# A recurrent attention and SoLU feed-forward kernel gets a new written-out order of work: u spread by a bf16 product, no dummy products, more loads issued by GpSimd, more transposes by DMA

## The chip, the cores and the metric

The kernel runs on one core of a Trainium2 chip. The metric is the device time of one execution in microseconds (us); the time of a kernel is the median of its runs. A core has five engines that run beside one another, each through its own list of instructions in order: PE (TensorE, products), DVE (VectorE), ACT (ScalarE), POOL (GpSimd) and SP (SyncE, which here only issues transfers). PEld in the profile is PE's loading of weights. Transfers (DMA) are issued from SP, ACT or POOL. PSUM is the memory that PE writes to, in eight banks; POOL does not read it here.

## The reference, cut to what matters

```
B, H, S, D = 4, 8, 768, 48                       # batch, heads, sequence, head width
for t in range(S):                               # recurrence, for each b, h
    cur = (u * k[t]) outer v[t]
    y[t] = r[t] @ (state + cur)
    state = w[t][:, None] * state + k[t] outer v[t]
x = y as rows of 384 (8 heads x 48), 3072 of them
h = x @ w_in                                     # 384 -> 1024
solu = h * softmax(h)                            # along 1024
ln = (solu - mean) / sqrt(var + 1e-6) * g_ln     # along 1024
out = ln @ w_out                                 # 1024 -> 384, float32
```

## The kernel before, in words

The sequence is cut into 6 chunks of 128 steps; a chunk of one batch entry is a unit, so there are 24 units, numbered chunk by chunk (units 0 to 3 are the first chunk of the four batch entries). All eight heads of a unit are handled together; rows are the 128 steps.

A unit goes through these stages, each a small function with a two- or three-letter word (line numbers of the kernel before in brackets):

- Loads of w, k, r, v, 192 KB each: `LW`, `LK`, `LR`, `LV` (264 to 275), into rings of seven buffers (`NIO`).
- `lw` takes the logarithm of w on ACT (338); `cum` sums it along the steps by two products on PE (341); `ex` is the exponential on ACT, in place in PSUM (347); `kp` scales k and r by it on DVE (351).
- `krk` and `krr` turn k and r by eight transposes on PE (380), and `kr` copies them from PSUM on ACT or DVE (395). `kt` does all of this by one DMA transpose issued from SP (399).
- `M` forms the scores by eight products (408), `m` copies them and cuts them to the lower triangle on DVE, or copies them on ACT and leaves the triangle to POOL's `sel` (416, 425).
- The u term: `p` = k times r and `q` = p times u on POOL (355, 359), `dg` sums q over a head on DVE (372), `dv` = v times dg on POOL (376). `vb` is v in bf16, by ACT or POOL (368).
- `Y` is the attention output: products with the state of the chunk before and with v (430). With `.i` an identity product on PE adds dv and `y` is a copy on ACT; with `.n` the addition is part of `y` on DVE (452).
- `S` forms the state's increment (458), `et` its decay on ACT, `st` the new state on DVE (482). With `S.n` an identity product that adds the old state is left out and `st` is two DVE instructions, a sum and a product.
- `X` and `xT` turn y by three transposes and a copy (491, 496); `xt` does it by a DMA transpose from SP (402).
- `H` is the hidden product (503), `e` its exponential on ACT, `he` the product of both on DVE, `hq` its square, mostly on ACT. Units named by an `ht` word have the hidden product by rows, and a DMA turns their result (405).
- `Oa`, `Ob` are the output product (584): for each of eight blocks one product of 386 columns with the prepared w_out, one of two columns with e and one of one column with hq. `ea` and `qa` (529, 550) let POOL add the two halves of e or of hq first, so that four small products do for eight.
- `qm`, `lv`, `rs` form the scale of a row, `o` applies it on ACT or DVE, `out` stores 192 KB from SP (630 to 665). Unit 23's hidden stage is split in halves (`HA`, `HB` and so on, 554).

Once, at the start, come: `us`, `uc`, u as a row spread over 128 partitions by an fp32 product and copied (290, 294); `gs`, `gc`, the gain turned (297); `wi`, w_in in bf16 (304); `gw`, `mn`, `mc`, `ce`, w_out times the gain, its column mean, and the mean taken off (308 to 328); `ih`, `ik`, constants made by POOL (243, 255); and `hot`, dummy products of 512 columns that nobody reads (330).

The order of the work is written out in one string, `ORDER` (line 21), of some 880 words: stage, number, and after a dot how it is done. For loads this is the queue (none: SP, `a`: ACT, `g`: POOL), for computing stages the engine (`a`, `d`, `p`) or the PSUM bank. The words are run one after another (line 680), and each engine's instructions stand in the order in which the words name them, loads included:

```
queue = {"": sp, "a": act, "g": pool}
...
for word in ORDER.split():
    word, _, how = word.partition(".")
    name = word.rstrip("0123456789")
    stages[name](int(word[len(name):]), how)
```

Every instruction is recorded through one helper, so nearly all have line 86 in the profile; they are told apart by tiles: `kp`, `m`, `y`, `he` and so on by the names above, `w` for the prepared w_out, `ps` for PSUM.

Of the kernel before, what the change touches and what calls it, by code (L numbers as in the profile page):

```python
# [8 lines left out]
F32 = mybir.dt.float32  # L9
BF16 = mybir.dt.bfloat16  # L10
# [15 lines left out]
m3.d p2 st0 cum6.0 dg3 gw0.a cum5.4 ex4 S3.7 gw1.a p4 kp4 q2 dv3 krr1 ex6 dg1 LV5.g krk4.3 krr4 ex5 vb1.a Y0.i2  # L26
kp6 kr4.d y0.a LI2 et3 X0.2 krk6.3 st3 p6 kr1.a vb2.a LW8 xT0.a kp5 krr6 LI0.a dg2 M1.0 krk5.7 krr5 kr6.a m1.d
S1.2 dv1 M4.4 dv2 Y3.i3 S2.6 gw4.a LK7 gw7.a et2 kr5.d LW7.g et1 m4.d hot1.7 y3.a gw5.a gw6.a p5 LR7.g M6.0
vb5.p Y2.i7 Y1.n3 vb4.a mn0.4 wi1.a y2.a st1 LW11.a wi0.p mc0 m6.d st2 S4.5 X3.2 LW10 y1.d et4 wi2.p ce0.d xT3.a
S5.0 ce5.p X1.7 LW9.a LV7.g et5 X2.6 M5.2 lw7 st5 st4 cum7.0 xT2.a H0.5 xT1.a LR10 lw8 ex7 m5.d ce1.d e0 H1.2  # L30
LR8 kp7 q5 he0 H3.0 q4 LV8.a ce3.p lw10 dg5 ce7.p ce6.p krk7.5 dg4 LK10 H2.6 LK8.a LV11 ce2.p krr7 LV6 e1 Y4.n4
he1 hq0.a LW13.a e3 e2 ce4.p dv4 he3 Oa0.3 cum10.1 he2 kr7.d y4.d Ob0 p7 cum8.6 qm0 lw11 hq1.a dv5 Oa1.0 ex10
Y5.n5 kp10 LR11 y5.d p8 LK11.a LK13 LW15 Ob1 X4.5 ex8 M7.1 lv0 krk10.4 rs0 kp8 q6 o0.a LK9.a vb6.p LW12 LR9 qm1
krr10 hq3.a dg6 cum11.6 q8 m7.d xT4.a Oa3.5 LV9.a lv1 out0 rs1 o1.a kr10.d out1 vb7.p vb8.a q7 ex11 LR12.g S7.0
LK12.a dv6 hq2.a LR14.g dg7 H4.2 et7 LK15.g lw9 e4 dg8 lw12 Ob3 kp11 st7 dv7 p10 krk8.1 qm3 cum9.6 Oa2.4 ex9 lv3
he4 Y7.n0 krr8 rs3 LW14.a o3.a Y6.n2 hq4.a kp9 y7.d LR17.g S6.3 Ob2 y6.d kr8.d p9 LW17 et6 X5.7 st6 LW19 qm2
LV12.a X7.2 krk11.6 vb9.a krr11 LR13 cum12.0 krk9.5 out3 xT7.d krr9 LK17 LK14 xT5.a lw15 lv2 kr11.d M8.2 q10 rs2
ex12 H5.6 o2.d q9 m8.a kp12 dv8 M11.3 lw13 S8.0 kr9.d m11.d p11 M9.1 LW16.a Oa4.5 e5 Ob4 m9.a et8 ea5.p he5
LR15.a X6.2 st8 vb11.p xT6.d sel8 out2 M10.3 p12 lw14 kt12 lw17 qm4 LV10 cum13.6 cum14.1 hot2.0 m10.d Y8.n0 S9.3
LR16.g hq5.a ex14 LW20 sel9 dg9 lv4 kp14 ex13 LW18.a Oa5.4 rs4 cum17.1 o4.a kp13 S11.5 y8.d et9 out4 cum15.6 Ob5  # L40
kt14 ex17 et11 ex15 Y9.n0 kp17 vb10.a H6.1 qm5 q11 dv9 lv5 rs5 LV15.g kp15 X8.6 st9 dg11 LR18.g y9.d LK16 o5.a
# [15 lines left out]
y19.d lv14 out15 y20.d ht16 LV23 ea17.p vb22.p rs14 vb21.a o14.a H18.0 p23 e18 X20.2 dg22 M22.3 S19.7 hq17.a
kp23 xT20.d m22.d Oa16.6 sv16 dv21 Y21.n5 hq16.a sv18 vb23.a Ob16 sq16 et19 H20.2 out13 he18 q23 y21.d dg23 dv22
e20 st19 xt19 he20 H19.0 Y22.n5 Oa17.7 kt23 e19 dv23 qm16 Ob17 y22.d ht18 M23.4 xt21 he19 lv16 rs16 o16.d Oa18.3
Ob18 hq20.a H21.0 hq18.a hq19.a m23.d ht20 xt22 out14 sq18 sv20 qm18 e21 lv18 ea19.p Y23.n2 rs18 Oa19.6 qm17  # L60
ea21.p lv17 rs17 y23.d Ob19 he21 Oa20.5 hq21.a qm19 out16 H22.0 o17.d xt23 lv19 o18.d rs19 Oa21.2 HA23.3 Ob21
# [39 lines left out]
def kernel(  # L101
# [14 lines left out]
    C = 128  # L116
# [50 lines left out]
    u_row = consts.tile([1, DM], F32)  # L167
# [29 lines left out]
    ones_row = consts.tile([1, C], F32)  # L197
    dve.memset(ones_row, 1.0)
# [37 lines left out]
    u_bc = consts.tile([C, H, D], BF16)  # L236
    gr = consts.tile([128, KF], F32)
# [38 lines left out]
    def load_u(i, x):  # L276
        queue[x].dma_start(out=u_row, in_=u.rearrange("(o h) d -> o (h d)", o=1))
# [436 lines left out]
```

## Time and profile before

| what | value |
|---|---|
| median of 3 runs | 143.97 us (143.61 to 146.4) |
| the profiled execution | 142.83 us |
| its span, first to last instruction | 141.0 us |
| PE, DVE, ACT, POOL busy in the span | 125.5, 122.3, 118.9, 118.3 us |
| moved by DMA | 31.98 MB, 227 GB/s in the mean |
| loads issued by POOL | 31 |

A row of grouped instructions has line, engine, operation, output<-inputs, shapes and count, then busy us of the group, mean ns of one, and the idle time just before them with what ended it. A row of the timeline has start, duration, engine, what, and in brackets the idle time before it. Busy times of neighbours overlap: the ends of products are modelled, so the step from one start to the next is the better price of a product in a stream.

### The profile page before, as it was taken

How to read it: one execution, taken by the hardware profiler on the slowest of the kernel's cores; microseconds unless marked ns; L12 is line 12 of the kernel's file. 1: busy time of each engine (PE TensorE's matmuls, PEld its weight loads, DVE VectorE, ACT ScalarE, POOL GpSimd, SP SyncE). 2: the span in 40 equal slices, each digit the busy share in tenths (PEclk: the TensorE clock that was granted, in tenths of full speed). 3: DMA queues.
4: the chain of work that ended last, by engine and by line, in shares of the span. 5: the costliest groups of instructions: out<-in, count | busy, mean ns of one | idle time of the engine just before them, and what ended most of it. 6: DMA issues, size and time to landing. Idle time of an engine off the chain costs nothing.

```text
span 141.0 us, 4797 instructions
## 1 busy us (share of the span) xinstructions
PE 125.5 (89%) x1890; PEld 94.6 (67%) x1890; DVE 122.3 (87%) x202; ACT 118.9 (84%) x243; POOL 118.3 (84%) x152
## 2 busy tenths in 40 slices
PE   0597956978999999999999999999999999999960
PEld 0136535657967887669877788788867766788740
DVE  6048879997999999999999998999999999878750
ACT  3648799979999999999989979998767889897780
POOL 7999999989999999999999999999999984402300
PEclk9999999999999999999999999999999999999996
DMA  4999999999999999999999999999999499652324
GB/s 89 274 298 343 323 278 388 382 307 232 263 234 237 285 297 295 242 227 223 297 190 238 188 242 213 291 224 162 186 228 213 97 255 86 144 170 78 123 73 154
DMA packets 94569, 31.98 MB, mean 227 GB/s; under 512 B 88569, under 2 KB 92674, under 8 KB 94546
## 3 DMA queue, kind: packets, MB, share of 16 engines
q1 hardware_dynamic: 70578, 20.92, 69.9%
q10 hardware_dynamic: 21984, 4.65, 15.6%
q0 software_dynamic: 1984, 6.10, 14.5%
q8 instruction: 15, 0.25, 0.8%
q14 instruction: 8, 0.07, 0.2%
HBM read 22.03 MB, written 4.72 MB: 190 GB/s over the span
## 4 chain that ended last, share of the span: by engine, by line
PE 40%; POOL 15%; DMA 13%; DVE 8%; ACT 5%; issue 2%; SPq 0%; ACTq 0%; POOLq 0%
PE ps L86 40%; DMA win_f<-in_moe_w_in_dram 5%; DMA kr_in<-in_k_dram 5%; DMA xT<-y 3%; POOL w L86 3%; POOL q L86 3%; DVE m L86 2%; POOL dv L86 2%; DVE he L86 2%; POOL m L86 2%; DVE y L86 1%; POOL win_sb L86 1%; ACT ps L86 1%; DVE kp L86 1%; POOL v_in L86 1%
## 5 line engine op out<-in xcount | busy, mean ns | idle before, releaser
L86 PE MATMUL ps<-w,he 128*128 128x386 bf16 (+1 forms) x192 | 43.2, 324 | 0.0
L86 PE MATMUL ps<-xT,win_sb 128*128 128x128 bf16 x504 | 31.2, 219 | 0.4 <-DMA xT<-y 0.2
L86 PEld LDWEIGHTS <-win_sb 128*128 128x128 bf16 x504 | 29.0, 98 | 2.1 <-DMA xT<-y 0.4
L86 ACT ACTIVATE e<-ps 128x1024 bf16<-128x1024 f32 (+1 forms) x25 | 24.6, 986 | 6.6 <-PE ps L86 5.0
L86 DVE TENSOR_TENSOR kp<-ps,kr_in 128x768 bf16<-128x768 f32 x24 | 22.7, 951 | 7.4 <-DMA kr_in<-in_r_dram 3.8
L86 PE MATMUL ps<-one_col,hq 128*128 128x1 bf16 x168 | 27.4, 163 | 0.0
L86 DVE TENSOR_TENSOR he<-ps,e 128x1024 bf16<-128x1024 f32 (+1 forms) x22 | 25.6, 1170 | 1.6 <-ACT e L86 1.3
L86 DVE TENSOR_TENSOR m<-ps,keep 128x1024 bf16<-128x1024 f32 x22 | 26.6, 1216 | 0.4 <-PE ps L86 0.4
L86 POOL TENSOR_TENSOR p<-kr_in 128x384 bf16<-128x384 f32 x24 | 24.0, 1004 | 0.3
L86 ACT ACTIVATE hq<-he 128x1024 bf16<-128x1024 bf16 (+1 forms) x21 | 21.6, 1030 | 0.7 <-DVE he L86 0.7
L86 POOL TENSOR_TENSOR q<-p,u_bc 128x384 bf16<-128x384 bf16 x24 | 21.7, 914 | 0.1
L86 POOL TENSOR_TENSOR dv<-vb,dg 128x384 bf16<-128x384 bf16 x24 | 19.8, 831 | 2.1 <-DVE dg L86 1.9
L86 ACT ACTIVATE ps<-ps 128x768 f32<-128x768 f32 x24 | 18.9, 796 | 2.6 <-PE ps L86 2.4
L86 PEld LDWEIGHTS <-he 128*128 128x128 bf16 x192 | 18.1, 96 | 3.5
L86 PEld LDWEIGHTS <-hq 128*128 128x128 bf16 x168 | 14.5, 96 | 8.8
L86 POOL TENSOR_TENSOR ea<-e 128x512 bf16<-128x512 bf16 x9 | 10.3, 1151 | 8.3 <-ACT e L86 8.3
L86 ACT ACTIVATE lw<-w_in 128x384 bf16<-128x384 f32 x24 | 12.3, 520 | 4.9 <-DMA w_in<-in_w_dram 4.9
L86 PE MATMUL ps<-inv_col,e 128*128 128x2 bf16 x96 | 15.8, 165 | 0.0
L86 PEld LDWEIGHTS <-kp 128*128 128x128 bf16 x176 | 11.8, 102 | 3.6 <-DVE kp L86 1.9
L86 PEld LDWEIGHTS <-kr 64*128 64x128 bf16 (+1 forms) x272 | 10.2, 95 | 5.3 <-issue 1.9
L86 DVE TENSOR_REDUCE dg<-q 128x8 f32<-128x384 bf16 x24 | 12.8, 544 | 0.2 <-POOL q L86 0.2
L86 DVE TENSOR_TENSOR st<-ps,et 128x384 bf16<-128x384 f32 x20 | 10.9, 549 | 0.6 <-ACT et L86 0.6
(97 smaller groups left out, 271.8 us busy)
## 6 DMA issues: line engine op xcount, KB each, us to landing
out_dram<-o SPq DMA_DIRECT2D x24, 192.0 KB, 3.7
kr_in<-in_k_dram SPq DMA_DIRECT2D x13, 192.0 KB, 5.8
kr_in<-in_r_dram POOLq DMA_DIRECT2D x12, 192.0 KB, 4.8
w_in<-in_w_dram SPq DMA_DIRECT2D x11, 192.0 KB, 5.2
kr_in<-in_r_dram SPq DMA_DIRECT2D x10, 192.0 KB, 4.8
v_in<-in_v_dram SPq DMA_DIRECT2D x10, 192.0 KB, 5.7
v_in<-in_v_dram POOLq DMA_DIRECT2D x9, 192.0 KB, 4.3
w_in<-in_w_dram ACTq DMA_DIRECT2D x8, 192.0 KB, 3.6
```

Source lines behind the costliest of these rows:

```text
L86: made = make(*args, **kwargs)
```

## The change

The string `ORDER` is replaced as a whole. What the new one does:

| | before | after |
|---|---|---|
| first units of the order | 3, 0, 1, 2 | 1, 2, 0, 3 |
| `hot` words (dummy products) | 5 (15) | 0 |
| loads of w, k, r, v by POOL | 5, 5, 12, 9 = 31 | 8, 11, 11, 10 = 40 |
| by ACT | 8, 6, 2, 5 = 21 | 8, 5, 3, 6 = 22 |
| by SP | 11, 13, 10, 10 = 44 | 8, 8, 10, 8 = 34 |
| k, r turned by DMA (`kt`) | 12 units | 14 units |
| `kr` copies on ACT, DVE | 4, 8 | 6, 4 |
| y turned by DMA (`xt`) | 10 units | 12 units |
| `xT` copies on ACT, DVE | 11, 3 | 7, 5 |
| units by rows (`ht`) | 16, 18, 20 | 17, 20 |
| `Y.i` with `y` on ACT | 4 | 9 |
| `S.n` | 0 | 6 |
| `ea` on POOL | 9 | 6 (14, 16, 18, 19, 21, 22) |
| `qa` on POOL | 0 | 6 (the same units) |
| `wi` on ACT, POOL | 1, 2 | 3, 0 |
| `ce` on DVE, POOL | 2, 6 | 3, 5 |
| `vb` on ACT, POOL | 14, 10 | 15, 9 |
| `o` on ACT, DVE | 18, 6 | 16, 8, one of them shared by both (unit 23, stored in two halves) |

u is loaded as eight rows of 48. DVE multiplies them by the identity, which gives a tile with u's rows on the block diagonal, and a bf16 product with ones spreads it. The transposed form of that tile is made as well (`uk`, `ud`). New functions for a sum of p times u on PE (`PT`, `pt`, `pd`, `DG`) are added, but no word of the new order calls them, and they alone would read the transposed form.

```diff
 ORDER = """
-LU0 LR3.g LW3.a LW1.a LW2.g lw3 LR0.a cum3.0 LG0 ih0 ex3 LW0 gs0.7 LK3 LR2.g hot1.2 LV0.g ik0 LK0 lw1 lw0 LV3.g
-gc0 cum0.4 LK2.a us0.6 p0 lw2 LW5.g ex0 kp3 LR1 kp0 cum1.0 cum2.2 krk3.7 krr3 uc0 ex2 q0 ex1 kp2 LK1 LR6.g kp1
-krk0.6 LW4 krr0 krk2.5 krr2 kr0.a lw4 LR4.g vb0.a kr2.d vb3.a p1 M0.3 p3 LO0 LW6 dg0 M2.5 kr3.a LK4 m0.d lw5
-hot10.1 LV1 LR5 LK6.a dv0 LK5.g m2.d LV2.a LO1 M3.0 S0.7 q3 gw2.a gw3.a hot1.4 LI1 q1 lw6 krk1.6 cum4.2 et0 LV4
...
+LW2.a LW0.a LW1 LK0.a LV0.a ih0 LW3.g lw1 LR3.g LU0 LK1.g ub0 LR0 uk0.3 lw2 LV1 lw0 LR2.g us0.1 uc0 LK3 LK2.g
+ud0.a LV3.g cum0.0 lw3 ex0 LR1 kp0 LW4.g cum3.2 LW6.a cum1.6 p0 LV2 ex3 LW5.g LR4.g kp3 ex1 q0 p2 vb0.a cum2.1
+ex2 kp1 LG0 krk3.5 krk0.7 ik0 krr3 krr0 kp2 kr0.d krk1.4 LW7.a dg0 krk2.0 LK6.a LV4 q2 M0.1 kr3.a LR5.g lw6 m0.d
...
+xT0.d mn0.5 st2 wi0.a LK10 xT1.a m4.d LV5.g LK9.g LR10 mc0 m5.d cum7.0 dg4 q5 ex7 kp7 LR12.a H0.6 ce2.p lw10
+ce6.d LW12.a e0 H1.2 ce1.p krk7.4 vb10.a ce4.p krr7 LR9.g vb5.p he0 LV9.g dv4 vb7.p LK11 e1 kr7.a H3.0 ce3.d he1
+e3 H2.6 ce0.p Y4.n3 ce5.p ce7.d S5.4 S7.5 hq1.a e2 lw8 q6 he3 LV8.g LR11.a et7 p7 LK8 p8 cum10.1 Oa1.0 ex10 Ob1
...
+H20.2 rs14 q23 o14.d kt23 dv22 Y21.n1 hq18.a Ob16 dv21 y22.d ea18.p y21.d H19.4 st19 out14 Oa17.7 LV23.g e20
+he20 e19 hq20.a Ob17 he19 qa18.p Oa18.2 ea19.p xt21 out15 sq17 Ob18 dg23 qm17 M23.4 qm16 vb23.p xt22 hq19 dv23
...
-    u_row = consts.tile([1, DM], F32)
+    u_rows = consts.tile([H, D], F32)
...
-    ones_row = consts.tile([1, C], F32)
-    dve.memset(ones_row, 1.0)
+    ones_rows = consts.tile([H, C], BF16)
+    dve.memset(ones_rows, 1.0)
...
-        queue[x].dma_start(out=u_row, in_=u.rearrange("(o h) d -> o (h d)", o=1))
+        queue[x].dma_start(out=u_rows, in_=u)
...
+    def diagonal_u(i, x):
+        dve.tensor_mul(out=u_diag, in0=u_rows.unsqueeze(1).to_broadcast([H, H, D]),
+                       in1=ident_f[:H, :H].unsqueeze(2).to_broadcast([H, H, D]))
+
+    def turn_u(i, x):
+        ps["uk"] = bank([128, KM, H], BF16, x, "uk_ps")
+        for j in range(KM):
+            pe.transpose(ps["uk"][:, j, :], u_diag.rearrange("k h d -> k (h d)")[:, j * 128:(j + 1) * 128],
+                         ident[:H, :H])
+
+    def copy_turned_u(i, x):
+        copy = {"a": act.copy, "d": dve.tensor_copy}[x]
+        copy(out=u_cols, in_=ps["uk"])
+
     def spread_u(i, x):
         ps["u"] = bank([C, DM], F32, x, "u_ps")
-        pe.matmul(ps["u"], lhsT=ones_row, rhs=u_row, start=True, stop=True)
+        pe.matmul(ps["u"], lhsT=ones_rows, rhs=u_diag.rearrange("k h d -> k (h d)"), start=True, stop=True)
```

More of the change, by code (lines that the diff above doesn't have):

```diff
@@ L27 @@
[L27 to L41, printed above, removed]
@@ L57 @@
[L57 to L61, printed above, removed]
@@ L65 @@
+qm18 lv17 lv16 lv18 m23.d ht20 H21.0 Y23.n3 qa19.p rs16 H22.4 e21 o16.d rs17 y23.d o17.d e22 rs18 Oa19.6 he21
+Oa20.7 xt23 he22 out16 ea21.p Ob20 ea22.p Ob19 o18.d hq21.a HA23.5 out18 qm19 sq20 out17 hq22.a lv19 qa21.p rs19
+HB23.0 sv20 qm20 Oa21.4 EA23 o19.d qa22.p Ob21 EB23 DA23 Oa22.6 lv20 Ob22 out19 QA23.a DB23 rs20 qm21 o20.a
+Oa23.2 out20 QB23.d qm22 lv22 rs22 lv21 Ob23 rs21 o21.d out21 qm23 o22.a lv23 rs23 o23.d out22 out23.h
 """
@@ L236 @@
     u_bc = consts.tile([C, H, D], BF16)
+    u_diag = consts.tile([H, H, D], BF16)
+    u_cols = consts.tile([128, KM, H], BF16)
     gr = consts.tile([128, KF], F32)
@@ L370, in v_cast, with turned, bonus_turn, bonus_turn_copy @@
         copy(out=vb_t[i % NLW], in_=v_t[i % NIO][:, :, :D])
+    def turned(i):
+        return q_t[i % 3].rearrange("t h d -> t (h d)").rearrange("t (j n) -> t j n", j=KM)
+    def bonus_turn(i, x):
+        p_ps = live[i]["p_ps"] = bank([128, KM, C], BF16, x, "p_ps")
+        for j in range(KM):
+            pe.transpose(p_ps[:, j, :], p_t[i % 3].rearrange("t h d -> t (h d)")[:, j * 128:(j + 1) * 128], ident)
+    def bonus_turn_copy(i, x):
+        copy = {"a": act.copy, "d": dve.tensor_copy}[x]
+        copy(out=turned(i), in_=live[i]["p_ps"])
+    def bonus_turn_dma(i, x):
+        sp.dma_start_transpose(out=turned(i), in_=p_t[i % 3].rearrange("t h d -> t (h d)"))
+    def bonus_product(i, x):
+        dg_ps = live[i]["dg_ps"] = bank([C, H], F32, x, "dg_ps")
+        for j in range(KM):
+            pe.matmul(dg_ps, lhsT=turned(i)[:, j, :], rhs=u_cols[:, j, :], start=(j == 0), stop=(j == KM - 1))
     def bonus_sum(i, x):
+        if "dg_ps" in live[i]:
+            copy = {"a": act.copy, "d": dve.tensor_copy}[x]
+            copy(out=dg_t[i % NWK], in_=live[i]["dg_ps"])
+            return
         part = slice(0, D // 2) if i in halved else slice(0, D)
@@ L667 @@
     stages = dict(
+        ub=diagonal_u, uk=turn_u, ud=copy_turned_u, PT=bonus_turn, pt=bonus_turn_copy, pd=bonus_turn_dma,
+        DG=bonus_product,
         ih=make_halves, ik=make_keep, LW=load_w, LK=load_k, LR=load_r, LV=load_v, LU=load_u, LG=load_g, LI=load_w_in, LO=load_w_out,
```

50 lines of the change are left out of this document (31 added, 19 removed).

## The prediction

> **What bounds the kernel now.** I read the page's totals first, then the busy time of the engines in four stretches, then the chain that ended last, then single rows. A first fence from the page: busy times, and the slices of GpSimd (POOL).
>
> ```profile
> PE 125.5 (89%) x1890; PEld 94.6 (67%) x1890; DVE 122.3 (87%) x202; ACT 118.9 (84%) x243; POOL 118.3 (84%) x152
> ...
> POOL 7999999989999999999999999999999984402300
> ```
>
> Four engines are within 7 us of one another, so the mean says nothing; the stretches do. Columns: the stretch, its length, then busy us of each engine, the granted clock, DMA.
>
> ```profile
> 12.00:38.80 26.80, 21.85 (x346) 16.54 (x344) 24.74 (x34) 24.38 (x48) 26.30 (x32) 1.00 1.14 315
> 38.80:82.30 43.50, 42.82 (x705) 33.58 (x700) 42.94 (x68) 41.29 (x83) 43.03 (x52) 1.00 1.17 247
> 82.30:136.50 54.20, 54.08 (x822) 41.14 (x822) 49.65 (x77) 45.65 (x101) 38.32 (x43) 1.00 0.87 173
> 136.50:141.00 4.50, 0.00 (x0) 0.00 (x0) 0.25 (x1) 0.98 (x3) 0.00 (x0) 0.70 0.40 148
> ```
>
> Until 38.8 POOL is full (26.30 of 26.80) and PE has 5 us to spare. From 38.8 to 136.5 PE idles 0.68 + 0.12 = 0.8 us in 97.7. The last 4.5 us are one unit's scaling and store. The chain agrees, and single rows of POOL and PE show where the stretches meet.
>
> ```profile
> 23.15 6.93 DMA win_f<-in_moe_w_in_dram
> ...
> 37.92 1.68 POOL w L86 x2
> ...
> 82.33 54.11 PE ps L86 x822
> ...
> 137.26 0.58 ACT o L86
> ```
>
> ```profile
> 35.57 4.04 POOL L86 TENSOR_TENSOR w<-w,mean_sb 128x384 bf16<-128x384 bf16 x5
> ```
>
> ```profile
> 38.82 0.32 PE L86 MATMUL ps<-w,he 128*128 128x386 bf16 x1
> ```
>
> The first output product (`Oa0`) starts at 38.82, when the fourth of POOL's five centrings in that row is through (four fifths of 4.04 past 35.57: 38.8). So the time is: POOL's work ahead of that centring, plus PE's work behind it, plus the tail. I forecast each of the three.
>
> **The change, part by part.**
>
> *POOL ahead of the first output product.* Durations of POOL's instructions:
>
> ```profile
> L86 POOL DMA_DIRECT2D kr_in<-in_r_dram x12 | 11.1, 921 | 0.3 <-POOL p L86 0.3
> L86 POOL CAST win_sb<-win_f 128x1024 bf16<-128x1024 f32 x2 | 2.0, 1041 | 0.3 <-DMA win_f<-in_moe_w_in_dram 0.3
> L86 POOL TENSOR_TENSOR w<-w,mean_sb 128x384 bf16<-128x384 bf16 x6 | 4.9, 835 | 0.0
> L86 POOL TENSOR_TENSOR ea<-e 128x512 bf16<-128x512 bf16 x9 | 10.3, 1151 | 8.3 <-ACT e L86 8.3
> L86 POOL TENSOR_TENSOR dv<-vb,dg 128x384 bf16<-128x384 bf16 x24 | 19.8, 831 | 2.1 <-DVE dg L86 1.9
> L86 POOL CAST vb<-v_in 128x384 bf16<-128x384 f32 x10 | 4.9, 498 | 0.7 <-DMA v_in<-in_v_dram 0.6
> ```
>
> A load costs POOL 0.92 us of its own time. In the new order `Oa1` is first and waits for `ce0`. Ahead of the end of `ce0` POOL has 18 loads where 13 stood ahead of `ce2`; 5 dv for 4; 2 v casts for 1; 4 centrings for 5; and the two casts of w_in are gone (ACT has them). That is 5 x 0.92 + 0.83 + 0.50 - 0.84 - 2 x 1.04 = +3.0 us: the first output product at 41.8. Below this, POOL's 0.3 us wait for w_in may go; above, `Ob1` waits one centring more (0.8). I take 3.0, with -0.3 and +0.8 as ends.
>
> *PE behind it.* Starts of consecutive rows give the step of a stream:
>
> ```profile
> 100.23 1.50 PE L86 MATMUL ps<-xT,win_sb 128*128 128x128 bf16 x24
> 101.67 0.40 PE L86 MATMUL ps<-kr 64*128 64x128 bf16 x8
> 102.00 0.18 PE L86 MATMUL ps<-off_blocks,halves 128*128 128x8 bf16 x1
> ...
> 102.47 0.33 PE L86 MATMUL ps<-st,kr 128*128 128x96 bf16 x4
> ```
>
> A 128-column product steps 1.44/24 = 0.06. Two more k, r turned by DMA remove 16 transposes (0.96), two more y 6 (0.36). One state (102.00 to 102.47) and one cumulate move ahead of the first output product: 0.47, and as estimate 0.4 for the two products. Six more y carry an identity product and six states drop theirs, equal columns, so 0. The small products (20 more of e, 16 fewer of hq, in 2 columns or 1) and the unit that goes from rows to columns come to +0.1. The dummies and the old u product:
>
> ```profile
> L86 PE MATMUL ps<-warm 128*128 128x512 bf16 x15 | 4.3, 395 | 0.2 <-DVE kr L86 0.2
> L86 PE MATMUL ps<-u_row,ones_row 1*128 1x384 f32 x2 | 1.6, 923 | 0.0
> ```
>
> Two of fifteen dummies lie behind 38.8 (0.57 at most, 0.4 taken). The other thirteen and the u product lie in the stretch with 5 us of PE idle: worth 0. The new u path (one product on DVE, three small transposes, one bf16 product, two copies) is ready long before POOL reaches `q0`, which stands behind seven loads and a product: 0 as well; the transposed copy of u has no reader in this order. Behind: -0.96 - 0.36 - 0.47 - 0.4 - 0.4 + 0.1 = -2.5. PE ends at 41.8 + 97.7 - 2.5 = 137.0, 0.5 later than the 136.5 of now.
>
> *Tail.* The last scaling, 0.58 on ACT, is halved between ACT and DVE and its store between two queues: -0.3 at most, since half the columns don't halve a short instruction. I take -0.3, with 0 as the other end.
>
> *DVE and ACT.*
>
> ```profile
> L86 DVE COPY kr<-ps 128x1024 bf16<-128x1024 bf16 x8 | 5.5, 682 | 0.0
> L86 DVE TENSOR_TENSOR st<-ps,et 128x384 bf16<-128x384 f32 x20 | 10.9, 549 | 0.6 <-ACT et L86 0.6
> L86 DVE TENSOR_TENSOR y<-ps,dv 128x384 bf16<-128x384 f32 x20 | 10.8, 549 | 0.3 <-issue 0.3
> L86 ACT COPY kr<-ps 128x1024 bf16<-128x1024 bf16 x4 | 4.1, 1017 | 0.2 <-PE ps L86 0.2
> L86 ACT CAST y<-ps 128x384 bf16<-128x384 f32 x4 | 1.9, 484 | 0.0
> L86 ACT CAST win_sb<-win_f 128x1024 bf16<-128x1024 f32 x1 | 1.1, 1057 | 0.0
> ```
>
> DVE: four copies of kr fewer (-2.7), five y fewer (-2.7), six states add a sum before their product (+3.3; this product of an fp32 tile in SBUF is not in the trace: the rows here bound six of them by 3.3 and, at POOL's 0.83, 5.0); the smaller moves (two o, two xT, one centring, u) are of this size each and positive. Sum +0.5 to +3, taken +0.7. ACT: two kr (+2.0), five y (+2.4), two casts (+2.1), less four xT and two o: about +3.4. From 38.8 on DVE idles 5.1 and ACT 10.8, so both are covered; if DVE had no cover, its 0.7 would be the price.
>
> *Start.* The first four scalings of k, r set DVE off:
>
> ```profile
> 11.39 1.91 DVE L86 TENSOR_TENSOR kp<-ps,kr_in 128x768 bf16<-128x768 f32 x2 [0.60 <-ACT ps L86]
> ```
>
> They end at 13.3 now. In the new order w3, r3, k1, r2, k2 are POOL's loads, behind the seven instructions of `ih0`, and `lw3` stands ahead of `ex0` on ACT. Five loads of 0.92, from some 4 us on as estimate, and another 4 to land put k2 at 12.6 to 13, so the four end near 13.9: +0.6, hidden, since POOL and not DVE releases the first output product.
>
> *The end of POOL's list.* The last dv, and what it meets:
>
> ```profile
> 119.49 0.83 POOL L86 TENSOR_TENSOR dv<-vb,dg 128x384 bf16<-128x384 bf16 x1 [1.95 <-DVE dg L86]
> ...
> 126.72 1.15 POOL L86 TENSOR_TENSOR ea<-e 128x512 bf16<-128x512 bf16 x1 [3.96 <-ACT e L86]
> ```
>
> ```profile
> 125.99 0.56 DVE L86 TENSOR_TENSOR y<-ps,dv 128x384 bf16<-128x384 f32 x1 [0.30 <-issue]
> ```
>
> ```profile
> v_in<-in_v_dram POOLq DMA_DIRECT2D x9, 192.0 KB, 4.3
> ```
>
> POOL was ready for `dv23` at 117.5. Now nine more loads (8.3), three more adds of squares, priced as ea (3.5), two fewer ea (-2.3), two casts, a centring and a v cast fewer (-3.4) stand ahead: +6.1, 123.6. `LV23` is POOL's too, and its cast stands only two adds (2.3) behind it where landing takes 4.3: 2.0 of waiting with `dv23` and the last adds queued behind. It ends at 126.4; `y23`, at 125.99 + 0.5, needs it at 126.5. Price 0, cover 0.1.
>
> *Turning by DMA.* Four more transposes on SP, and ten loads fewer there; whoever waits is a score or a hidden product several units later in the order. Price 0; without that cover one landing, 4.8 by the kr rows' kind, would show.
>
> The Trainium skill ("DMA: Bandwidth & Descriptors", Issuing engines are not separate DMA queues) says that another issuing engine saves only sequencer time, as all share 16 DMA engines. By that rule the nine moved loads gain nothing in transfer; the POOL rows add that here they cost the issuer 0.92 each.
>
> **Sum.** The profiled execution took 142.83 (span 141.0 and 1.8 around it): 142.83 + 0.5 - 0.3 = 143.0. The median of the runs, 143.97, lies 1.14 above it: **144.2**.
>
> **Rivals.** *POOL becomes the bound (slower).* Each us that POOL waits ahead of `dv23` beyond 0.1 goes through to the end. Four ea and three adds of squares now stand ahead of it, and each waits for ACT; one wait like the 3.96 above gives 148.0. It decides (over 2%) from 2.9 us of such waits. Against it: behind 82 us the present waits fell after the last dv, when PE had nothing else. Chance 0.22.
>
> *The clock falls without the dummies (slower).* Early and later transposes, and the end of the run:
>
> ```profile
> 10.32 1.86 PE L86 MATMUL ps<-ident,kp 128*128 128x128 bf16 x16
> 12.41 0.62 PE L86 MATMUL ps<-ident,kp 128*128 128x128 bf16 x8 [0.23 <-DVE kp L86]
> ```
>
> ```profile
> 135.00:141.00 6.00, 1.41 (x21) 0.77 0.36 134
> ```
>
> 0.116 us a step until about 12, 0.06 after; and a mean of 0.77 from 135 on means half rate from 138.2. Between 12 and 41.8 PE has 21.85 less the thirteen dummies (3.7): 18.1 us of work; all of it at half rate takes 35.0 of the 29.8 there are, and the first output product comes 5.2 later: 149.4. A slow stretch of a few us costs nothing, as 11.7 us are idle; it decides from 15.7 us of slow work on. The Trainium skill ("TensorE: Matmul & The Clock Gate", Why this matters for your kernels) asks for no gap over some 3 us; PE's 5 us of idle time between 12 and 38.8 are cut up by 346 products, so by that rule the clock stays up and the price is 0. Chance 0.10, at 149.4.
>
> *The start is not POOL's (faster).* If the centrings come as early as now because loads that POOL issues let everything ahead of them come sooner, -3.0, and if the 0.8 us of idle goes too, the time is 140.4. Against it: POOL is full from 12 on, and its order is fixed. Chance 0.09.
>
> **How the numbers follow.** My forecast has 0.59; its own range, 142.6 to 146.3, is from the ends above (-0.3, -0.8 of idle, -0.5 of PE's terms; +0.8, +0.3, +1 of DVE). Two per cent is 2.9 us, about what a measurement of this kernel can tell from no change: below 141.1 0.09, above 146.9 0.10 + 0.22. The range of 141.3 to 149.0 leaves out the faster case and the worst of the slow ones.
>
> **What would show it.** Right: the first output product at 41.5 to 42.6, PE without gaps from there to 136.5 to 137.5, POOL's last dv done near 126. Wrong: PE idle over 2 us behind the first output product (look at who ends it: ea or hq on POOL, a landing, a state), steps of 0.116 after 16 us, or the first output product at 39.

## The result, and the profile after

| | kernel before | changed kernel |
|---|---|---|
| median, runs on the same chip | 143.94 us (4 runs) | 149.73 us (148.61 to 150.51, 4 runs) |
| ratio to before, 95% interval | 1 | 1.0405 [1.0316, 1.0493] |
| profiled execution, its span | 142.83, 141.0 | 150.51, 148.8 |
| first output product, end of PE | 38.82, 136.4 | 43.26, 144.2 |
| tail behind PE | 4.6 | 4.6 |

The change costs 5.8 us, where 144.2 with 141.3 to 149.0 was forecast. In the experiments e5, e6, e15 and e17 below the profiled execution was a disturbed one (over 1.5% longer than the fastest of its kernel), so of e5, e6 and e17 only the ratio of the undisturbed runs is used, and e15, with one such run, has none.

The page of the changed kernel, busy times and the granted clock by slices (of before: nines up to a 6 in the last slice):

```profile
PE 125.3 (84%) x1874; PEld 95.5 (64%) x1876; DVE 128.7 (86%) x205; ACT 121.5 (82%) x245; POOL 127.4 (86%) x160
...
PEclk9999987978999999999999999999999999999998
```

The four stretches of the changed kernel, with the columns of the prediction's second fence:

```profile
12.00:38.80 26.80, 21.89 (x278) 16.67 (x278) 23.91 (x33) 23.38 (x45) 24.90 (x31) 0.87 1.13 320
38.80:82.30 43.50, 42.70 (x721) 33.88 (x719) 41.96 (x64) 42.19 (x83) 43.26 (x52) 1.00 1.19 241
82.30:136.50 54.20, 50.02 (x779) 38.38 (x779) 52.37 (x73) 43.60 (x91) 44.95 (x50) 1.00 0.91 166
136.50:149.00 12.50, 7.75 (x94) 5.44 (x92) 6.71 (x14) 7.07 (x21) 3.46 (x3) 0.93 0.34 126
```

Two things are new. From 82.3 to 136.5 PE idles 54.20 - 50.02 = 4.2 us where it idled 0.1, and DVE has 1.8 us to spare there where it had 4.55. And POOL is not full before 38.8: 24.90 of 26.80. Rows of the changed kernel at both places, from its timeline by engine:

```profile
43.26 0.33 PE L85 MATMUL ps<-w,he 128*128 128x386 bf16 x1
```

```profile
36.18 2.50 POOL L85 TENSOR_TENSOR w<-w,mean_sb 128x384 bf16<-128x384 bf16 x3 [1.70 <-ACT mean_sb L85]
```

```profile
10.94 2.01 DVE L85 TENSOR_TENSOR kp<-ps,kr_in 128x768 bf16<-128x768 f32 x2 [6.20 <-ACT ps L85]
13.30 2.00 DVE L85 TENSOR_TENSOR kp<-ps,kr_in 128x768 bf16<-128x768 f32 x2 [0.36 <-DMA kr_in<-in_r_dram]
```

```profile
9.69 0.52 ACT L85 ACTIVATE lw<-w_in 128x384 bf16<-128x384 f32 x1 [2.87 <-DMA w_in<-in_w_dram]
```

```profile
85.87 1.51 PE L85 MATMUL ps<-xT,win_sb 128*128 128x128 bf16 x24 [0.40 <-DMA xT<-y]
96.95 0.40 PE L85 MATMUL ps<-kr 64*128 64x128 bf16 x8 [0.85 <-DMA kr<-kp]
99.88 0.28 PE L85 MATMUL ps<-xT,win_sb 128*128 128x128 bf16 x2 [0.79 <-DMA xT<-y]
...
130.19 0.32 PE L85 MATMUL ps<-w,he 128*128 128x386 bf16 x1 [1.28 <-DVE win_f L85]
```

ACT's row is the wait that the forecast lacked: `lw3` stands ahead of `ex0` on ACT and waits for w3 until 9.69, so the first scaling starts at 10.94 and the fourth ends at 15.3 (13.3 before, 13.9 forecast). PE's three longest waits behind it (1.28, 0.85, 0.79) are ended by DVE, or by a transpose by DMA of a tile (kp, y) that DVE or ACT hands to it.

What PE waits for ahead of the first output product is another matter. A row of the timeline shows a wait from 0.15 us on, and the row of the first output product shows none, at 38.82 before as at 43.26 now. These are PE's last waits ahead of it, before and changed:

```profile
32.32 0.32 PE L86 MATMUL ps<-lw,uti_neg 128*128 128x384 bf16 x1 [1.33 <-ACT lw L86]
```

```profile
30.35 0.17 PE L85 MATMUL ps<-off_blocks,halves 128*128 128x8 bf16 x1 [0.55 <-ACT y L85]
```

From there PE works through its own list up to the first output product, 6.5 us before and 12.9 us now (3.4 of them at half the clock). In neither trace does a row show PE waiting for a centring.

Where the 7.8 us of the profiled execution's span went (it is the longest of its four; the medians differ by 5.8): first output product 43.26 - 38.82 = +4.4; PE's idle time from there to its end (all gaps between its rows added) from 0.7 to 5.0, +4.3; the rest of that stretch from 97.6 - 0.7 = 96.9 to 101.0 - 5.0 = 96.0, -0.9; tail 0.

The rows that explain most of the second part are DVE's groups by shape, changed kernel:

```profile
L85 DVE TENSOR_TENSOR st<-ps,et 128x384 bf16<-128x384 f32 x14 | 7.5, 549 | 0.8 <-ACT et L85 0.8
L85 DVE TENSOR_TENSOR st<-sn,et 128x384 bf16<-128x384 f32 x6 | 7.5, 1252 | 0.2
L85 DVE TENSOR_TENSOR sn<-ps,st 128x384 f32<-128x384 f32 x6 | 3.3, 551 | 1.2 <-ACT et L85 1.2
```

A product from PSUM takes 0.549 us, the same product of a tile in SBUF 1.252 in the mean. Look at three of the six beside POOL's rows (one fence for each engine, same times):

```profile
83.47 1.25 DVE L85 TENSOR_TENSOR st<-sn,et 128x384 bf16<-128x384 f32 x1
...
96.86 0.56 DVE L85 TENSOR_TENSOR st<-sn,et 128x384 bf16<-128x384 f32 x1
...
100.43 1.40 DVE L85 TENSOR_TENSOR st<-sn,et 128x384 bf16<-128x384 f32 x1
```

```profile
83.28 1.01 POOL L85 TENSOR_TENSOR p<-kr_in 128x384 bf16<-128x384 f32 x1
84.24 1.17 POOL L85 TENSOR_TENSOR dv<-vb,dg 128x384 bf16<-128x384 bf16 x1
...
96.85 0.92 POOL L85 DMA_DIRECT2D kr_in<-in_r_dram  x1
...
100.42 0.99 POOL L85 TENSOR_TENSOR p<-kr_in 128x384 bf16<-128x384 f32 x1
101.36 0.92 POOL L85 DMA_DIRECT2D kr_in<-in_k_dram  x1
```

At 83.47 DVE's product ends at 84.72, 0.43 behind the end of POOL's p (84.29); at 100.43 it ends at 101.83, 0.42 behind the end of p (101.41). At 96.86 POOL only issues a load, and the product takes 0.56. And POOL pays too: its dv, started at 84.24 while the product ran, takes 1.17 where dv takes 0.83. So the two seem to run one after the other. In e3 below a product takes 0.56 while POOL waits, and four of the other five end 0.42 behind the end of a POOL product. The Trainium skill ("SBUF — State Buffer", SBUF: two separate sides) states such a rule: a DVE operation with two SBUF inputs and a POOL operation that reads SBUF hold the shared port pair one at a time, for a whole instruction. The rows beside POOL's products agree with it. Those beside load issues do not agree with one another: 0.56 at 96.86, but the sixth product, at 126.85, starts beside a load issue and takes 2.15 us, to 0.4 behind POOL's next product, and in e3 one product has only load issues beside it and takes 0.94:

```profile
81.82 0.94 DVE L86 TENSOR_TENSOR st<-sn,et 128x384 bf16<-128x384 f32 x1
```

```profile
80.70 1.81 POOL L86 DMA_DIRECT2D kr_in<-in_k_dram  x2
82.50 0.88 POOL L86 DMA_DIRECT2D kr_in<-in_r_dram  x1
```

No run here explains these two. The sixth one matters: in the chain that ended last the sum at 126.36 and this product lead through DVE's next instruction to PE's wait of 1.28 at 130.19, its longest behind the first output product.

### The profile page after: what moved, and what is told of

Read it like the earlier page. It is cut to its first block, busy times and chain, and to the rows that moved or that the text cites. A ratio compares the mean times of both kernels' runs of the same rounds, so it can differ in the third digit from the quotient of the medians.

```text
span 148.8 us, 4765 instructions
## 1 busy us (share of the span) xinstructions
PE 125.3 (84%) x1874; PEld 95.5 (64%) x1876; DVE 128.7 (86%) x205; ACT 121.5 (82%) x245; POOL 127.4 (86%) x160
## 3 DMA queue, kind: packets, MB, share of 16 engines
q10 hardware_dynamic: 23312, 5.47, 16.7%
## 4 chain that ended last, share of the span: by engine, by line
PE 26%; DVE 14%; DMA 13%; ACT 10%; issue 3%; ACTq 1%; DVEq 0%
PE ps L85 26%; DMA kr<-kp 7%; DMA xT<-y 3%; ACT ps L85 3%; DMA v_in<-in_v_dram 3%; DVE he L85 3%; DVE st L85 2%; DVE kp L85 2%; DVE m L85 2%; ACT hq L85 1%; DVE dg L85 1%; ACT lw L85 1%; DVE sn L85 1%; DVE y L85 1%; ACTq L85 1%
## 5 line engine op out<-in xcount | busy, mean ns | idle before, releaser
L85 PE MATMUL ps<-w,he 128*128 128x386 bf16 (+1 forms) x192 | 42.9, 325 | 1.3 <-DVE win_f L85 1.3
L85 PE MATMUL ps<-xT,win_sb 128*128 128x128 bf16 x528 | 32.5, 219 | 1.4 <-DMA xT<-y 1.2
L85 PEld LDWEIGHTS <-win_sb 128*128 128x128 bf16 x528 | 30.1, 98 | 2.9 <-DMA xT<-y 1.5
L85 DVE TENSOR_TENSOR he<-ps,e 128x1024 bf16<-128x1024 f32 (+1 forms) x23 | 26.7, 1169 | 0.6 <-ACT e L85 0.4
L85 PE MATMUL ps<-one_col,hq 128*128 128x1 bf16 x152 | 24.4, 163 | 0.1
L85 ACT ACTIVATE hq<-he 128x1024 bf16<-128x1024 bf16 (+1 forms) x22 | 22.8, 1041 | 1.8 <-DVE he L85 1.5
L85 PE MATMUL ps<-inv_col,e 128*128 128x2 bf16 x128 | 20.6, 165 | 0.0
L85 PEld LDWEIGHTS <-he 128*128 128x128 bf16 x192 | 17.0, 96 | 2.3
L85 PEld LDWEIGHTS <-kr 64*128 64x128 bf16 (+1 forms) x272 | 11.4, 99 | 6.6 <-issue 2.4
L85 PE MATMUL ps<-lw,uti_neg 128*128 128x384 bf16 x24 | 9.0, 374 | 4.8 <-ACT lw L85 4.0
L85 PE MATMUL ps<-kr 64*128 64x128 bf16 x192 | 10.6, 232 | 2.7 <-ACT gr L85 1.2
```

What stands on the lines that cost most here:

```text
L85: made = make(*args, **kwargs)
```

## The experiments

Ratios are to the kernel before, on the same chip. Theory A: the six states' sums by DVE, with products that exclude POOL. Theory B: DVE's idle time covers them. Theories D (clock), S, P and V (what sets the start) as named below.

**The six states.** Four kernels. e1, in the changed kernel:

```diff
-S12.n1 S14.n1 S16.n5 S18.n7 S17.n4 S19.n7
+S12.1  S14.1  S16.5  S18.7  S17.4  S19.7
```

> The changed kernel, with the six states 12, 14, 16, 17, 18, 19 summed by an identity product in the bank again, as the other states are. Theory A (the product of two SBUF operands on DVE and POOL's work exclude each other): the six products fall from 1.25 us to 0.55, the six sums go, so DVE's busy time falls by 7.5 us from 128.7 to about 121, PE gains 1.0 us, and the time falls from 149.7 to 144.5 to 146.5. Theory B (the start and POOL's nine loads make the whole loss, DVE has cover): within 1 us of 149.7.

1.0311 [1.0235, 1.0387], median 147.69. DVE's busy time falls to 122.0 and its products to 0.550, as A has it, but the time falls by some 2 us, not 3 to 5. Its rows say why: PE ends at 141.9, 2.3 earlier, and the first output product still comes at 43.38.

```profile
82.30:136.50 54.20, 52.22 (x812) 40.36 (x812) 48.60 (x70) 45.50 (x95) 46.45 (x52) 1.00 0.90 171
```

From 82.3 to 136.5 PE idles 2.0 us instead of 4.2, and DVE has 5.6 us to spare.

e2, in the changed kernel, the sum written back to its bank:

```diff
-            dve.tensor_add(out=sn_t[i % 2], in0=total, in1=st_t[b][(c - 1) % 2])
-            total = sn_t[i % 2]
+            dve.tensor_add(out=total, in0=total, in1=st_t[b][(c - 1) % 2])
```

> The changed kernel, with the sum of the six states written back to their bank in PSUM instead of to a tile in SBUF: the same twelve instructions on DVE, but the product reads one operand from PSUM. Theory A: the products take 0.55 us each instead of 1.25 (DVE's busy time about 124.5), POOL's dv and p beside them go back to 0.83 and 1.0, and the time falls by 2 to 4 us to 145.5 to 147.5. Theory C (it is the second instruction that costs, wherever the sum lies): the products still take about 1.25 us, time within 1 us of 149.7. Theory B (start and loads): products at 0.55, but time within 1 us of 149.7.

1.0295 [1.0215, 1.0376], median 148.25; products at 0.551, DVE 124.9. With six sums still on DVE it can't be told from e1: the second instruction doesn't show. The intervals of e1 and e2 overlap that of the changed kernel, so the cleaner pair is made in the kernel before. e3 has its six states summed as in the changed kernel (`S12.1` to `S12.n1`, and so for 14, 16, 17, 18, 19), e12 the same with the edit of e2.

> The kernel before, with nothing changed but that its states 12, 14, 16, 17, 18, 19 are summed by DVE through a tile in SBUF. Theory A: the six products take 1.0 to 1.5 us, DVE's busy time rises by 6 to 9 us from 122.3, which is more than the 4.6 us that DVE idles from 82 to 136 us, and the time rises by 2 to 5 us from 144.0. Theory B (DVE's idle time covers it): within 1 us of 144.0.

> The kernel before, with states 12, 14, 16, 17, 18, 19 summed by DVE, but the sum written back to PSUM (through a tile in SBUF it took 149.6 us, 5.9 over the kernel before, with products of 0.93 us). Theory A (the product of two SBUF operands waits for POOL): products at 0.55 us, DVE's busy time 3.3 over that of before, time 145.5 to 147.5. Theory C (a second instruction in a full DVE is what costs): products at 0.55, but the time still 148.5 or more.

e3: 1.0426 [1.0345, 1.0507], median 149.58. e12: 1.0137 [1.0029, 1.0245], median 145.84. DVE's groups of e3, then of e12, then the last full stretch of each:

```profile
L86 DVE TENSOR_TENSOR st<-sn,et 128x384 bf16<-128x384 f32 x6 | 5.6, 926 | 0.2
L86 DVE TENSOR_TENSOR sn<-ps,st 128x384 f32<-128x384 f32 x6 | 3.3, 545 | 0.0
```

```profile
L86 DVE TENSOR_TENSOR st<-ps,et 128x384 bf16<-128x384 f32 x20 | 11.0, 552 | 0.4 <-ACT et L86 0.2
L86 DVE TENSOR_TENSOR ps<-ps,st 128x384 f32<-128x384 f32 x6 | 3.3, 558 | 0.0
```

```profile
82.30:136.50 54.20, 49.43 (x733) 37.22 (x733) 51.89 (x75) 40.72 (x88) 38.44 (x43) 0.97 0.82 163
```

```profile
82.30:136.50 54.20, 52.43 (x789) 39.38 (x790) 51.18 (x79) 43.45 (x96) 38.32 (x43) 1.00 0.83 169
```

The same twelve instructions cost 2 us through PSUM and 6 through SBUF. In e3 PE idles 4.8 us in that stretch (e12: 1.8). Theory A is shown, B and "the extra instruction" are not; sizes lie a little outside A's ranges (products at 0.93 where 1.0 to 1.5 was expected, 5.9 us where 2 to 5 was). The six products alone added 2.3 us to DVE's busy time. Of the rest of the 3.7 us between e3 and e12 up to 1.7 can be the clock: in e3 it is at half rate for 3.4 us from 102.8 on, with PE busy, and in e12 it isn't. That the rest lies in what waits for those states is argued, not shown. In the changed kernel the same six cost less; why is not shown.

**The clock.** e4 puts seventeen dummies back into the changed kernel (its two ahead of unit 2's state write zeros over half of the scores of unit 6); e8 takes the fifteen out of the kernel before.

```diff
-cum1.6        cum2.1        krk0.7        gs0.7        X2.4        S2.0
+hot1.7 cum1.6 hot2.7 cum2.1 hot1.7 krk0.7 gs0.7 hot5.6 hot6.6 X2.4 hot2.6 S2.0
```

> The changed kernel with seventeen dummy products of 512 columns put back where PE idles in the first 31 us (one ahead of the second cumulate, two ahead of the third, one ahead of the transposes of unit 0, five behind the turning of g, six and two between 27 and 30.5 us). Theory D (the clock, without the dummies, is what makes the first output product late): full clock from about 14 us, none of the two stretches at half rate, first output product at 41.0 to 42.0 instead of 43.3, time lower by 1 to 2 us. Theory B (POOL's list alone sets it): clock full, but the first output product at 43 and the time within 0.6 us of 149.7.

```diff
-hot1.2 ... hot10.1 ... hot1.4 ... hot1.7 ... hot2.0
```

> The kernel before without its fifteen dummy products of 512 columns, nothing else changed (their results are read by nothing). Theory D (the clock needs them): stretches at half rate between 12 and 39 us, and because of them the first output product later than 38.8 by 1 us or more and the time up by as much, 145 or more. Theory B (PE has 5 us to spare there and POOL sets the first output product): it stays at 38.5 to 39.2 whether the clock falls or not, time 143.4 to 144.6.

e4: 1.0483 [1.0404, 1.0563], first output product at 43.23. e8: 1.0014 [0.9969, 1.0058], at 38.57. The clock rows of e4 and e8:

```profile
PEclk9999999999999999999999999999999999999996
```

```profile
PEclk9999758999999999999999999999999999999996
```

With dummies the clock is full and the time is not lower; without them it falls, in the kernel before too, and the time is the same. D's mechanism exists and doesn't show in the time of these two. It is not free wherever it falls: e2 has the start of e1 word for word, but PE is at half rate from 27.0 to 33.8 us and has no wait from 28.4 to 42.6, and its first output product comes at 44.59, 1.2 behind e1's. One trace each; how much of the 1.2 is the clock is not shown.

**The start.** First w3, the first load of POOL, in the changed kernel: by ACT (e5), with e1 (e6), with e1 and five more loads of POOL by SP (e7, which alone has the second edit).

```diff
-LW3.g
+LW3.a
...
-LW5.g LR4.g LR5.g LK5.g LW8.g
+LW5   LR4   LR5   LK5   LW8
```

> The changed kernel, with one load moved: w of unit 3, the first load that POOL issues, is issued by ACT's queue at the same word. Theory S (w3 lands late by POOL, lw3 stands ahead of ex0 on ACT, and so DVE's first scaling starts at 10.9 us and DVE is late for POOL's dv and for the mean; this start and not POOL's list alone makes the first output product late): the first scaling starts at 7 to 9 us, POOL loses its 1.7 us wait ahead of the centrings as well as one load, and the first output product comes at 40.5 to 41.5 instead of 43.3. DVE stays full behind it, so of the 2 to 2.5 us some part (1 to 2.5) shows in the time: 147.2 to 148.7. Theory P (POOL's list alone): one load less, first output product at 42.3, time 148.7 to 149.7.

> The changed kernel with both: w of unit 3 issued by ACT, and the six states summed by the identity product in the bank (147.7 us alone). Theory S with A (the two causes lie one behind the other and add up): first output product at 40.5 to 41.5, DVE's busy time 121 to 122, time 145.0 to 146.2. If they don't add up, because something else holds the end (POOL's list): 147 to 148.

> As the run before, and five more of POOL's loads ahead of the first output product (w5, r4, r5, k5, w8) issued by SP. Theory P (what POOL issues ahead of the fourth centring sets the first output product, 0.92 us a load): it comes another 2.5 to 4.5 us earlier, at 37 to 38.5, and the time is 142 to 144. Theory S (the start sets it): at 40 to 41.5, and the time within 1 us of the run before.

Measured: 1.0461 [1.0318, 1.0605], 1.0257 [1.015, 1.0364], 1.0332 [1.0225, 1.0439]. e7 misses both of its cases, e5 lies above both (its interval reaches into P's), e6 lies in its second. In e7 the fourth scaling ends at 16.75 and the first output product comes at 43.96, with six loads fewer on POOL. So theory P is wrong for e7, and theory S is not tested by these three: the start came later and not earlier. The queue was not what made w3 late: as fifth transfer of ACT's queue it comes later still (ACT's `lw3` starts at 11.14 in e7, at 9.69 in the changed kernel). So it was put second on SP's queue (e9), with e1 (e10), and with e1 and the five loads (e11): `LW1 LW3` at the head, no `LW3.g`.

> The changed kernel, with w of unit 3 loaded by SP as its second transfer, behind w1, instead of by POOL as the ninth transfer or so. By the run before last the place in the row of transfers counts, not the queue: from 2 us on the DMA engines are full (about 250 GB/s, 0.79 us for 192 KB). Theory S (the late w3 delays DVE's first scaling, and DVE the first output product): the first scaling at 7 to 9 us instead of 10.9, POOL without its 1.7 us wait, and with a load less, first output product at 40.6 to 41.6, time 147.5 to 149 (DVE full behind it). Theory P (POOL's list alone): first output product at 42.3, time 149 to 150.

> The same with the six states summed by the identity product in the bank (147.7 us alone). If late start and sums by DVE are two causes one behind the other: first output product at 40.6 to 41.6 and the time 145.0 to 146.2. If the start costs nothing: 147 to 148.

> The same, and five more of POOL's loads ahead of the first output product (w5, r4, r5, k5, w8) issued by SP. With the start on time POOL's list is what is left: theory P: first output product at 37.5 to 39.5, time 142 to 144. If, as in the run with w3 on ACT, DVE is still late: first output product at 41 to 43 and the time within 1 us of the run before.

1.0436 [1.0359, 1.0513], 1.025 [1.0165, 1.0335], 1.039 [1.0314, 1.0467]. e9 and e11 miss, e10 is as if the start cost nothing, and has the lowest ratio of the changed kernel's variants, at 147.44. w3 is early now, but k and r of the next units are later: the fourth scaling ends at 17.2, 16.8 and 16.7. In e9 and e10 it ends 1.9 and 1.5 us later than in the changed kernel, and the first output product comes at 43.2 and 43.0, no later: within this order the fourth scaling does not set it.

Then a two by two on e1: five loads off POOL (e13), three centrings `ce3`, `ce6`, `ce7` from DVE to POOL (e15), both (e14), and both with the loads of v0 and v1 behind r1 (e16).

> The changed kernel with the six states summed by the identity product (147.7 us alone, first output product at 43.38) and five of POOL's loads ahead of the first output product (w5, r4, r5, k5, w8) issued by SP; w3 stays with POOL. Theory P (POOL's list alone): first output product 3 to 4.5 us earlier, at 39 to 40.5, time 143.5 to 144.7. Theory V (DVE: fourth scaling at 15.2, then 27.6 us of work): unchanged at 43 to 44, time 147 to 148.5.

> As the run before, and three centrings (columns blocks 3, 6, 7 of w_out) computed by POOL instead of DVE: 1.8 us less on DVE, 2.5 us more on POOL, which has 4.6 us from the five loads. Theory V: the first output product 1.5 to 2 us earlier than in the run before, at 41.2 to 42.2, time 145.2 to 146.5. Theory P: 2.5 us later than in the run before.

> The six states summed by the identity product, all POOL loads as in the changed kernel, and the three centrings computed by POOL. Theory P or both engines side by side: POOL's list is 2.5 us longer, first output product at 45 to 46, time 149.5 to 150.5. Theory V alone: 41.5 to 42.5, time 146.

> As the second run (five loads by SP, three centrings by POOL), and the loads of v0 and v1 issued by SP behind r1 instead of as fourth of ACT's and fourth of SP's transfers; 0.79 us each on full DMA engines. The fourth scaling of k, r should end at 13.6 to 14.4 instead of 15.2. Theory V: the first output product comes 0.8 to 1.6 us earlier than in the second run, at 40 to 41.4, and the time is 144.0 to 145.5. If POOL's list is then the limit: within 0.4 us of the second run.

e13: 1.0377 [1.0327, 1.0427], e14: 1.048 [1.0406, 1.0555], e16: 1.039 [1.0331, 1.0449]; e15 is inconclusive (147.01 to 154.79). First output products at 43.99, 44.97 and 44.72: theory P is wrong for e13, whose product comes when V has it, and theory V for e14 and e16. P's other sizes miss as well (1.0 later in e14 where 2.5 was expected, and e16 is 1.3 us below e14). In e14 and e16, where POOL does three more centrings, PE waits for one, as in no other trace of the table below; in e14:

```profile
44.97 0.32 PE L85 MATMUL ps<-w,he 128*128 128x386 bf16 x1 [0.98 <-POOL w L85]
```

Rows of DVE and then of POOL in e13:

```profile
23.18 0.96 DVE L85 TENSOR_TENSOR kp<-ps,kr_in 128x768 bf16<-128x768 f32 x1 [2.76 <-DMA kr_in<-in_k_dram]
```

```profile
26.74 1.62 POOL L85 TENSOR_TENSOR dv<-vb,dg 128x384 bf16<-128x384 bf16 x2 [5.87 <-DVE dg L85]
36.85 2.50 POOL L85 TENSOR_TENSOR w<-w,mean_sb 128x384 bf16<-128x384 bf16 x3 [0.25 <-ACT mean_sb L85]
```

POOL gave up 4.6 us of issuing and got 5.9 us of waiting: the loads now stand in SP's queue, k of unit 4 lands behind them, DVE scales it 2.8 us late, and POOL's dv waits for DVE.

Last, one of the two in the kernel before: v0 and v3 moved from POOL to the front (e17), and three loads moved from SP to POOL (e18).

```diff
-LW1.a ... LW0 ... LV0.g ... LV3.g        LW6 ... LK4 ... LR5
+LW1.a LV0.a ... LW0 LV3 (e17)            LW6.g ... LK4.g ... LR5.g (e18)
```

> The kernel before, with the loads of v0 and v3 moved from POOL to the front: v0 as third transfer of ACT's queue, v3 as fourth of SP's. POOL has two loads (1.8 us) less ahead of the first output product; the transfers of k, r behind them come up to 1.6 us later (0.79 us each on full DMA engines). Theory V (first transfers and DVE set the first output product): fourth scaling at 14.2 to 15.0 instead of 13.3, first output product at 39.7 to 40.5, time 144.5 to 145.5. Theory P (POOL's list sets it): fourth scaling late as well, but the first output product at 37.0 to 38.0, time 142 to 143.5.

> The kernel before, with three loads of its second half of the start (w6, k4, r5) issued by POOL instead of SP: 2.7 us more on POOL's list ahead of the first output product, nothing changed in the first ten transfers. Theory P: first output product at 41.3 to 41.8 instead of 38.8, time 146 to 147. Theory V: 38.6 to 39.4, time 143.4 to 144.6.

e17: 1.0181 [1.0086, 1.0276], slower by 2.6 us although POOL has 1.8 us less: the order of the first transfers costs, in V's direction and somewhat over its size, and P fails. e18: 1.0272 [1.0185, 1.0358], slower by 3.9 us, in P's direction and more; its first output product comes at 42.71. POOL and ACT in e18:

```profile
38.49 4.04 POOL L86 TENSOR_TENSOR w<-w,mean_sb 128x384 bf16<-128x384 bf16 x5
```

```profile
21.91 0.52 ACT L86 ACTIVATE lw<-w_in 128x384 bf16<-128x384 f32 x1 [3.57 <-DMA w_in<-in_w_dram]
```

The centrings start 2.9 us later than the 35.57 of before, the 2.7 us of issuing. But ACT also waits 3.6 us for w6, which lands later from POOL than it did from SP, and PE doesn't wait for a centring: its last wait, at 36.07, is for a state of DVE. So loads on POOL cost here, but not by the path that P names.

Fourth scaling, POOL's and PE's waits ahead of the first output product (rows of 0.15 us and more; for PE the last one, when it ends and what ends it), and the first output product, in us:

| | fourth scaling ends | POOL waits | PE's last wait ends | by | first output product |
|---|---|---|---|---|---|
| before | 13.3 | 0.3 | 32.3 | ACT lw | 38.8 |
| e18 | 13.4 | 0.7 | 36.1 | DVE st | 42.7 |
| changed | 15.3 | 1.7 | 30.4 | ACT y | 43.3 |
| e4 | 16.3 | 1.6 | 32.3 | DVE m | 43.2 |
| e1 | 15.2 | 1.6 | 32.5 | DVE m | 43.4 |
| e2 | 15.2 | 1.9 | 44.3 | DVE he | 44.6 |
| e9 | 17.2 | 2.4 | 42.9 | DVE he | 43.2 |
| e10 | 16.8 | 2.4 | 32.0 | DVE m | 43.0 |
| e11 | 16.7 | 8.6 | 35.1 | DVE kr | 45.0 |
| e13 | 15.2 | 6.3 | 43.7 | DVE he | 44.0 |
| e14 | 15.4 | 5.9 | 45.0 | POOL w | 45.0 |
| e16 | 14.5 | 5.7 | 44.7 | POOL w | 44.7 |

The waits at 42.9, 43.7 and 44.3 are of 0.2 us. e1 and e2 differ by 1.2 with the same start, so differences of that size between single traces show nothing. In e1, e4 and e10 PE's last wait ends about when it ended before, and 10.9 us of work follow where 6.5 did. What stands there in e1 stood ahead of PE's last wait in the kernel before:

```profile
32.45 0.40 PE L85 MATMUL ps<-kr 64*128 64x128 bf16 x8 [0.23 <-DVE m L85]
32.92 0.92 PE L85 MATMUL ps<-ident,y 128*128 128x128 bf16 x9
33.77 0.40 PE L85 MATMUL ps<-kr 64*128 64x128 bf16 x8
34.10 1.48 PE L85 MATMUL ps<-w,mean_w 128*128 128x384 bf16 x8
```

These are scores of two units, the turning of three units' y and the column mean of w_out: 3.0 us from 32.45 to 35.42. Behind 35.4 come the hidden products of four units, as before, and two states (1.1) and one cumulate (0.3) more.

## Why the prediction was wrong

*POOL ahead of the first output product, +3.0.* The size of POOL's own work is right: its fourth centring ends at some 43.0, 41.3 without the 1.7 us wait, so the work ahead of it grew by 2.8. The step that failed is the release: "The first output product (`Oa0`) starts at 38.82, when the fourth of POOL's five centrings in that row is through". It was read off two equal times, 38.8 and 38.82. PE's row has no wait there, and the chain that ended last, which was called in as agreeing, goes from POOL's centrings at 37.92 to POOL's next dv and a load, not to PE. PE's last wait in the kernel before is for the logarithm of w of unit 7, a load that POOL issues at 26.42; what follows is PE's own list. So POOL's list was close to PE's, but the sum ("POOL's work ahead of that centring, plus PE's work behind it, plus the tail") has no term for PE's work ahead of it, since PE had 5 us to spare until 38.8. Those 5 us lie up to the end of PE's last wait; behind it there were none, and in e1, e4 and e10 4.4 us more work stands there, as much as the 4.4 by which the first output product came late. The forecast did see one state and one cumulate move to this side (0.9), and took them off the other side only.

*The start, +0.6.* The fourth scaling ended 2.0 later, for w3 and not for k2: the forecast counted POOL's issues but not the order in which full queues deliver, nor what stands behind `lw3` on ACT. By e9 and e10 its end does not set the first output product. Between the two DVE is busy for 25.5 of 28.0 us (23.5 of 25.5 before); the 27.6 of theory V adds up durations of neighbours that overlap, so DVE's list was not full either.

*PE's idle time behind it stays 0.8.* This step failed too: 5.0. It stood on DVE's +0.7 being covered by 5.1 us of idle time, and the term under it that was mis-sized is the six products of a tile in SBUF: priced at 3.3, with 5.0 as the upper end, they took 7.5 (the six sums 3.3, as priced). DVE's busy time rose by 6.4, 4.2 of it from these products, and that is more than its cover. The nearest row was taken from an operation that reads PSUM, and an operation with two SBUF inputs has another neighbour: POOL, which was itself full. e3 against e12 shows it; in the changed kernel e1 and e2 bring back 2.0 and 1.5 us in the median, with intervals that overlap. The DMA transposes, priced at 0, end 2.0 us of PE's waits, but behind a late DVE: with the sums off DVE (e1) 0.3 us of them is left.

*PE's work behind it, -2.5.* 0.9 was seen, 1.6 short. In e1, where six identity products bring 1.0 back, the work is 95.9: -1.0 where -1.5 is due. So by e1 the sum of the parts is right within 0.7 (five more y carry an identity product and not six as the sum has it, so 0.2 more was due); where the other 1.1 of the changed kernel lies is not shown.

*Tail, -0.3:* 0, the other end.

*The rivals.* POOL as the bound gave nearly the time (148.0), but by luck, not by its mechanism: the last dv starts at 131.87 and ends 6.3 us behind the forecast 126.4, and PE has no wait from 130.19 to its end. e1 and e2 leave POOL's work as it is and PE's stalls shrink. The clock (149.4) is not the cause by e4 and e8: the mechanism took place, in two windows at half rate, without a cost in the time of these runs. The faster start did not occur.

*Open.* Why PE still had that work ahead of it at 32 us: the order of the words, the late start and the clock all bear on it, and no run moved PE's words alone. More loads on POOL (e18) and another order of the first transfers (e17) each made the kernel before slower, and in the changed kernel no relief of one list brought the first output product below some 43.0. None of these kernels beats the kernel before.

## What to carry to other kernels

An operand moved from PSUM to SBUF is a change of neighbours: price a two-SBUF-input operation on DVE by POOL's instruction beside it, and if a sum has to move to DVE, write it back to PSUM (2 us against 6 here). Where several engines and the DMA queues are all full, "hidden behind the fullest" is not a cover: compute each list's own end, PE's too, and count a moved load on the queue that gets it. Two equal times are not a release: look whether the row that starts shows a wait, and where its engine waited last, since idle time ahead of that wait covers nothing behind it. A wait that stands ahead on an in-order engine (`lw3` ahead of `ex0`) belongs into the forecast before any duration.

## What the runs showed of the hardware that was not expected

The clock fell without a long gap. Rows of PE in the changed kernel, half and full rate:

```profile
29.14 0.33 PE L85 MATMUL ps<-ident,y 128*128 128x128 bf16 x3 [1.38 <-DVE st L85]
...
31.87 1.21 PE L85 MATMUL ps<-ident,y 128*128 128x128 bf16 x9
33.01 0.61 PE L85 MATMUL ps<-kr 64*128 64x128 bf16 x8
...
35.75 2.84 PE L85 MATMUL ps<-xT,win_sb 128*128 128x128 bf16 x48
```

Nine transposes take 33.01 - 31.87 = 1.14, 0.127 each, where forty-eight products take 0.06 each four us later; the longest gaps in the 3.4 us ahead of this stretch were 1.38 and 0.55. The Trainium skill ("TensorE: Matmul & The Clock Gate", Why this matters for your kernels) gives gaps of over some 3 us as the danger; here the clock fell without one. What share of idle time it takes is not shown, and here PE was not waiting any more: it has no wait from 30.35 on.

On the start, the DMA engines are busy without a break (277 GB/s from 2 to 12 us in the changed kernel), and a load moved to another queue changed when others landed more than it changed the engine that issued it (e13: 4.6 us of issuing against 5.9 of waiting).
